# One core, a conditioned attention and MLP block: gate rows through memory, one token tile's maxima moved, the last products in another order

## The chip, the cores and the metric

The kernel runs on one core of one Trainium2 chip. The metric is the device time of one execution in microseconds (us), of the kernel before: median 770.49 of 3 runs (769.84 to 770.69).

## The reference

The block works on one sequence of S = 2048 tokens with D = 640 features, H = 32 heads of 20 features and an MLP of F = 1728. All inputs are float32.

```python
mod = (_silu(c) @ w_mod).reshape(c.shape[0], 6, 1, -1)
sa, ca, ga, sb, cb, gb = (mod[:, 0], ..., mod[:, 5])
h = _layernorm(x) * (1 + ca) + sa
# attention: q, k, v = h @ wqkv, per head
#   phi(u) = [softmax(u @ w_phi), softmax(-u @ w_phi)]
#   kv = phi_k^T v;  z = sum of phi_k over tokens
#   o = (phi_q kv) / (phi_q z + 1e-6);   A = o @ wo
x = x + ga * A
h = _layernorm(x) * (1 + cb) + sb
# MLP: r = max(h @ w1 + b1, 0);  B = (r * r) @ w2 + b2
x = x + gb * B
```

## The kernel before

**Numbers and tiles.** The tokens are cut into 16 tiles of 128 (index t), taken in 8 pairs (index j). Each float32 factor is split into a high part, rounded for TensorE, and a low part, the rest; a product is three matmuls (high by high, high by low, low by high). ScalarE writes the high part, VectorE subtracts it to get the low part (line 88, `lo`). So a product's third matmul, or its second, may wait for VectorE where its first waits for ScalarE.

**Stages.** Up to about 40 us weights are folded and the first tokens are normalized. Up to about 250 us a loop over t makes K, V and Q of each token tile (`proj`, tiles pk, pv, pq), the feature map's exponentials (ek, eq), and the sum kv (kvp). From about 250 to 385 us the attention output is made in a loop over j: TensorE turns the scaled features of a pair (ezb) in six groups (`tr_e`: tiles te 0 to 5, copied by ScalarE to ept 0 to 5; group 5 is the smallest, 80 rows), multiplies them with kv (`num`: tiles numa, numb, numc, for groups 0 and 1, 2 and 3, 4 and 5), and multiplies the outcome (ot) with wo (`do_wo`: pwo). ScalarE copies num's outcome as ot's high part (`num_hi`), VectorE makes ot's low part (`num_lo`). From 385 us on the MLP runs: for each pair j and each n = 0 to 6 two `up` products (f = 2n and 2n+1, h by w1, tile up), ReLU and square (ft), a split into ra, and the `down` products of an earlier n with w2 into accumulators. For the first pairs, and the last three n of the last pair, the down products are plain: four regions, named 2, 3, 4 and x, where 3 and x are the right 256 columns of the pair's two token tiles and 2 and 4 the left 384. Regions 3 and x lie in one bank of the accumulator memory (tile acc3x); 2 and 4 have one each.

**The gates and the other parts of mod.** mod has six parts of 640 numbers. `mod_mac(part, k)` adds row block k of w_mod, times silu(c), to a 128 by 640 sum on VectorE (tile wm), which needs one load of w_mod on SyncE's queue. A part that is wanted as a column (3 and 4, tile cols_b) is turned by five TensorE transposes (`mod_turn`: tile mc, or beside others in ta), copied by ScalarE (mt) and summed by VectorE (`mod_sum`). A part that is wanted as a row on all partitions (2 is the attention's gate, ga_b; 5 the MLP's, gb_b) is a matmul of the sum with a matrix of ones, in two halves (`mod_row`: tile mr, two matmul records each), and a copy on ScalarE.

**Order.** In the projection loop only TensorE's order is written out; a scheduler places the other engines' work. What is hung beside the loop stands in three tables by t: `SIDE`, `AFTER_KV` (behind the kv sum of a tile), and `LAST_COL` (the fifth transpose of a turn and its sum). From the attention loop on the order of all engines is the order of the program. VectorE's chain per pair there is the e' product with z (`e_prod`, into scr), its sums, and the scaling into ezb (`e_recip`, `e_scale`). Four token tiles are postponed or kept: their maxima, subtractions (`q_chain`) and exponentials are spread over j = 1, 3 and 5. In the MLP, tables `LN_AT0` to `LN_AT` say at which up product the next pair's adds and LN pieces are issued. The end is `last_downs`: the last n of the last pair, four regions, each with a gate multiply (`by_gate`), an add to y and a store.

Of the kernel before, what the change touches and what calls it, by code (L numbers as in the profile page):

```python
# [15 lines left out]
P = 128  # L16
S = 2048
D = 640
# [33 lines left out]
def kernel(  # L52
# [272 lines left out]
    def mod_row(part, dest, h, p=None):  # L325
        p = p or tp(f"mr{part}_{h}")
        c = slice(h * HALF, (h + 1) * HALF)
        nc.tensor.matmul(p[:, :HALF], ones, MA[part][:, c], start=True, stop=True)
        nc.scalar.activation(dest[:, c], p[:, :HALF], AF.Copy)
# [194 lines left out]
    def wo_weights(*gs):  # L524
# [4 lines left out]
        6: lambda: mod_turn(3, tp("mc3"), 0, 1, 2, 3),  # L529
        8: lambda: mod_row(2, ga_b, 0),  # L530
# [3 lines left out]
    LAST_COL = {7: (3, cols_b[:, 0:5]), 11: (4, cols_b[:, 5:10])}  # L534
    SIDE = {
        2: lambda: mod_mac(3, 0, 1, 2),
        3: lambda: (mod_mac(3, 3, 4), mod_mac(4, 0)),
        4: lambda: mod_mac(4, 1, 2),
        5: lambda: (mod_mac(4, 3, 4), mod_mac(2, 0)),
        6: lambda: mod_mac(2, 1, 2, 3),  # L540
        7: lambda: mod_mac(2, 4),
        8: lambda: None,
# [169 lines left out]
    for t in range(2, NT - 2):  # L712
        j, i = divmod(t, 2)
        if i == 0 and j < NT // 2 - 2:
            load_x(j + 2)
        PK[t] = row("s2", f"k{t}")
        to_sb(proj("k", t), PK[t])
        if t == NT - 4:
            t1(j + 1, 0, 1)
        if t == 9:  # L720
            mod_row(2, ga_b, 1)
        norm = j + 1 if i == 0 and t < NT - 4 else j + 2 if t == NT - 5 else None
        if norm:
            parts = ln_parts(XB[norm], f"a{norm}")
            with tc.issue_after(newest(ET_.Activation)):
                next(parts)
        p = proj("v", t, (1, 0, lambda: t1(j + 1, 4)) if t == NT - 3 else None)
        if i == 0:
            do_kv(t - 2)
            do_kv(t - 1)  # L730
            if t in AFTER_KV:
                AFTER_KV[t]()
        v_out(t, p)
        if norm:
            next(parts)
        EK[t] = tok2("k", f"ek{t}")
        spread(PK[t], EK[t], f"k{t}")
        exps(EK[t])
        if norm and not i:
            next(parts)  # L740
        if i and t < NT - 4:
            t1(j + 1, 2, 3)
        with tc.issue_after(newest(ET_.DVE)):
            k_norm(EK[t], t)
        if t < NT - POSTPONED:
            do_q(t, (1, 3, lambda: t1(j + 1, 4, more=LAST_COL.get(t))) if i else None)
            if norm and i:
                with tc.issue_after(newest(ET_.Activation)), tc.issue_after(DONE[0]):
                    next(parts)
            if i:  # L750
                with tc.issue_after(DONE[1]):
                    q_chain(t)
            else:
                q_chain(t)
        if i == 0 and t < NT - 4:
            t1(j + 1, 0, 1)
        SIDE[t]()
# [74 lines left out]
    def kv_diags():  # L832
# [3 lines left out]
        nc.tensor.transpose(kvt[1][:80, P : P + 40], kvs[:40, 600:680], ident[:40, :40])  # L836

# [275 lines left out]
    tr_e(0, range(3, NG))  # L1113
    mod_row(5, gb_b, 0, bank("mr5_0"))
    num(0)
    num_hi(0)
    mod_row(5, gb_b, 1, bank("mr5_1"))
# [11 lines left out]
    for j in range(NB):  # L1129
# [17 lines left out]
        def te(at):  # L1147
            for i, gs in enumerate((range(3), range(3, NG))):
                if nxt and te_at[i] == at:
                    tr_e(j + 1, gs)  # L1150
# [20 lines left out]
        if j == 3:  # L1171
            q_chain(KEPT + SPREAD[j], False)
# [17 lines left out]
        if j == 1:  # L1190
            q_chain(KEPT + SPREAD[j], False)
# [3 lines left out]
        if j in SPREAD:  # L1195
            exps(EQ[KEPT + SPREAD[j]])
        load_e(c + 2)
# [29 lines left out]
    def up(j, f):  # L1227

        n, k = FS[f], f % 2
        p = UP2[:, :256] if k and j < PLAIN else UP[:, 256 * k : 256 * k + 256]  # L1230
# [6 lines left out]
        mm(p, terms, first=(k == 0 or j < PLAIN), skip=True)  # L1237
# [204 lines left out]
    def last_downs(j):  # L1442
# [3 lines left out]
        for regs in ((("3", 0, R), ("x", 1, R)), (("2", 0, L),), (("4", 1, L),)):  # L1446
            for k in range(2):
                for r, i, c in regs:
                    f = NF - 2 + k
                    prod(j, r, block(j, NP - 1, (A11, A12, A21, A22)[2 * i + k]), W2[f], c, k == 1, FS[f])  # L1450
            for r, i, c in regs:
                m = c.stop - c.start
                t = u[:, at : at + m] if r != "4" else u[:, :m]
                at += m
                by_gate(t, acc(j, r)[1], c)
                add(Y[j][i][:, c], Y[j][i][:, c], t)
                store(j, i, c.start, c.stop)
# [11 lines left out]
    LN_AT2 = {"load": 0, "xx": 3, "add": (6, 7), "ln": (7, 8, 8, 8, 9, 9), 10: (0, 1), 11: (2, 3), 12: (4,)}  # L1469
# [45 lines left out]
    for j in range(NB):  # L1515
# [5 lines left out]
        for n in range(NP):  # L1521
            down = lambda k: prev and (down_plain if plain(*prev) else down_pair)(*prev, k)
            twice = not plain(j, n)
            m = NP * j + n - NP - 1
            done = j - 1 if j and prev else None
# [51 lines left out]
            if j == NB - 1 and n == NP - 1:  # L1577
                split_a(j, n, (0,))
                for i in range(2):
                    add(Y[j][i], Y[j][i], XR[j, i])  # L1580
# [3 lines left out]
            split_a(j, n, (0, 1) if (j, n) != (NB - 1, NP - 1) else (1,))  # L1584
# [89 lines left out]
```

## Time and profile before

| | |
|---|---|
| profiled execution, its own time | 770.42 us |
| its span, first to last instruction | 768.7 us |
| runs shown (3) | 769.84, 770.49, 770.69 us |
| mean clock granted to TensorE | 0.998 |
| TensorE matmuls busy | 760.7 us (99%) |
| VectorE busy | 591.4 us (77%) |
| ScalarE busy | 434.8 us (57%) |
| GpSimd busy | 146.8 us (19%) |

PE is TensorE's matmuls and PEld its weight loads, which run ahead of the matmuls; DVE is VectorE, ACT ScalarE, POOL GpSimd and SP SyncE. A row of a timeline has the start, the time from there to the end of the merged instructions, the engine, the line, the operation, what it writes and reads, and the number of instructions; in brackets stands how long the engine idled ahead of it, and what ended that. For weight loads, the distance between two starts is the time TensorE took for what lies between them.

### The profile page before, as it was taken

How to read it: one execution, taken by the hardware profiler on the slowest of the kernel's cores; microseconds unless marked ns; L12 is line 12 of the kernel's file. 1: busy time of each engine (PE TensorE's matmuls, PEld its weight loads, DVE VectorE, ACT ScalarE, POOL GpSimd, SP SyncE). 2: the span in 40 equal slices, each digit the busy share in tenths (PEclk: the TensorE clock that was granted, in tenths of full speed). 3: DMA queues.
4: the chain of work that ended last, by engine and by line, in shares of the span. 5: the costliest groups of instructions: out<-in, count | busy, mean ns of one | idle time of the engine just before them, and what ended most of it. 6: DMA issues, size and time to landing. Idle time of an engine off the chain costs nothing.

```text
span 768.7 us, 15287 instructions
## 1 busy us (share of the span) xinstructions
PE 760.7 (99%) x5965; PEld 740.3 (96%) x5965; DVE 591.4 (77%) x1081; ACT 434.8 (57%) x971; POOL 146.8 (19%) x301
## 2 busy tenths in 40 slices
PE   9999999999999999999999999999999999999997
PEld 9999999999999979988999999999999999999997
DVE  6698897968999899999556667866767666685656
ACT  5766756667853354556776647456463645546331
POOL 3001101202000255342101000222321313213110
PEclk9999999999999999999999999999999999999999
DMA  9711431512433355223356466897666759767450
GB/s 330 302 69 69 137 103 55 186 37 99 136 104 109 99 164 174 79 86 120 104 160 234 121 226 234 283 324 216 209 179 206 230 179 267 205 184 204 130 171 35
DMA packets 50551, 126.03 MB, mean 164 GB/s; under 512 B 5991, under 2 KB 6759, under 8 KB 50479
## 3 DMA queue, kind: packets, MB, share of 16 engines
q1 hardware_dynamic: 33144, 83.99, 31.8%
q0 software_dynamic: 14752, 35.76, 16.9%
q10 hardware_dynamic: 2583, 5.30, 1.8%
q8 instruction: 47, 0.77, 0.4%
q14 instruction: 25, 0.20, 0.1%
HBM read 95.05 MB, written 29.88 MB: 163 GB/s over the span
## 4 chain that ended last, share of the span: by engine, by line
PE 90%; DVE 4%; ACT 3%; DMA 1%; issue 1%; POOL 1%; SPq 0%; DVEq 0%; POOLq 0%; ACTq 0%
PE up L78 24%; PE acc L78 18%; PE pwo L78 10%; PE pk L78 7%; PE pq L78 7%; PE pv L78 6%; PE acc3x L78 5%; PE te L914 3%; PE kvp L450 2%; PE tb L357 1%; PE numa L78 1%; PE numb L78 1%; PE numc L78 1%; DMA wm<-in_w_mod 1%; PE foldk L280 1%
## 5 line engine op out<-in xcount | busy, mean ns | idle before, releaser
L78 PE MATMUL up<-h,w 128*128 128x256 f32 x1640 | 206.7, 278 | 0.2 <-ACT ft L1244 0.2
L78 PEld LDWEIGHTS up<-h,w 128*128 128x128 f32 x1640 | 196.2, 188 | 0.3 <-ACT ft L1244 0.3
L1244 ACT ACTIVATE ft<-up,b_t 128x256 f32<-128x256 f32 x104 | 48.8, 469 | 114.1 <-PE up L78 113.5
L78 PE MATMUL acc<-w,ra 128*128 128x384 f32 x452 | 98.0, 336 | 0.0
L1245 DVE TENSOR_TENSOR ft<-ft 128x256 f32<-128x256 f32 x104 | 44.1, 424 | 51.1 <-ACT ft L1244 49.5
L78 PE MATMUL pwo<-wo,ot 128*128 128x256 f32 (+3 forms) x512 | 81.1, 313 | 0.4 <-DVE ot L88 0.4
L78 PEld LDWEIGHTS pwo<-wo,ot 128*128 128x128 f32 (+1 forms) x512 | 74.4, 188 | 4.0 <-issue 2.7
L78 PE MATMUL pq<-wq,hT 128*128 128x384 f32 (+1 forms) x480 | 75.4, 312 | 0.0
L78 PEld LDWEIGHTS acc<-w,ra 128*128 128x128 f32 x452 | 72.7, 188 | 0.7 <-DVE ra L88 0.5
L78 PE MATMUL pk<-wk,hT 128*128 128x384 f32 (+1 forms) x480 | 72.7, 309 | 0.0
L78 PEld LDWEIGHTS pq<-wq,hT 128*128 128x128 f32 x480 | 71.2, 188 | 0.8 <-issue 0.2
L78 PE MATMUL pv<-wv,hT 128*128 128x384 f32 (+1 forms) x480 | 71.8, 307 | 0.0
L78 PEld LDWEIGHTS pk<-wk,hT 128*128 128x128 f32 x480 | 70.5, 188 | 0.4 <-issue 0.2
L78 PEld LDWEIGHTS pv<-wv,hT 128*128 128x128 f32 x480 | 70.0, 188 | 0.2
L88 DVE TENSOR_TENSOR ra<-ft,ra 128x384 fp32r<-128x384 f32 (+2 forms) x86 | 36.8, 449 | 32.9 <-ACT ra L1268 20.8
L78 PE MATMUL acc3x<-w,ra 128*128 128x256 f32 x248 | 42.4, 279 | 0.0
L1354 POOL DMA_DIRECT2D ring_a<-td_a x34 | 18.2, 536 | 124.7 <-PE acc L78 102.4
L1268 ACT ACTIVATE ra<-ft 128x384 fp32r<-128x384 f32 x48 | 25.2, 525 | 28.4 <-DVE ft L1245 22.4
L78 PEld LDWEIGHTS acc3x<-w,ra 128*128 128x128 f32 x248 | 39.8, 188 | 0.2 <-DVE ra L88 0.2
L878 POOL TENSOR_TENSOR dn<-dn,rs_q 128x32 f32<-128x32 f32 x32 | 22.6, 706 | 66.6 <-DVE dn L872 66.3
L441 DVE TENSOR_REDUCE sk<-ek 128x64 f32<-128x1280 f32 x16 | 23.7, 1483 | 13.9 <-ACT ek L436 13.4
L1259 DVE TENSOR_TENSOR ft<-ft 128x128 f32<-128x128 f32 x136 | 33.3, 286 | 1.2
(263 smaller groups left out, 1405.2 us busy)
## 6 DMA issues: line engine op xcount, KB each, us to landing
ring_c<-td_c POOLq DMA_DIRECT2D x34, 384.0 KB, 4.0
ring_a<-td_a POOLq DMA_DIRECT2D x34, 384.0 KB, 4.0
ring_b<-td_b POOLq DMA_DIRECT2D x34, 256.0 KB, 3.6
esp<-eq SPq DMA_DIRECT2D x12, 640.0 KB, 3.1
el<-esp SPq DMA_DIRECT2D x12, 640.0 KB, 5.3
rw<-in_w SPq DMA_DIRECT2D x23, 320.0 KB, 3.4
wm<-in_w_mod SPq DMA_DIRECT2D x20, 320.0 KB, 3.8
xb<-in_x SPq DMA_DIRECT2D x8, 640.0 KB, 4.0
```

What stands on the lines that cost most here:

```text
L78: nc.tensor.matmul(o, a, b, start=first and i == 0, stop=last and i == len(terms) - 1, skip_group_check=skip,)
L88: (eng or nc.vector).tensor_tensor(out_lo, full, hi.bitcast(F32), op=ALU.subtract)
L280: nc.tensor.matmul(p[g // 3][:, (g % 3) * 120 : (g % 3) * 120 + n], r, bd_t[:120, g * 120 : g * 120 + n], start=True, stop=True,)
L441: nc.vector.tensor_reduce(s, heads(flat(e)), axis=AX.X, op=ALU.add)
L450: nc.tensor.matmul(kvp[g // 4][64 * c : 64 * c + 64, a : a + 2 * n].rearrange("p (s n) -> p s n", s=2), v[:, u], e[:, :, o : o + n], start ...
L878: nc.gpsimd.tensor_tensor(dn[:, s], dn[:, s], rs[:, 1 - s], op=ALU.mult)
L914: nc.tensor.transpose(p[:m, a : a + P], EU[2 * j + i][:, b : b + m], ident)
L1244: nc.scalar.activation(r, p, AF.Relu, bias=b1_t[:, f : f + 1])
L1245: nc.vector.tensor_tensor(r, r, r, op=ALU.mult)
L1259: nc.vector.tensor_tensor(t[:, o], t[:, a], t[:, b], op=op)
L1268: nc.scalar.activation(a[:, 0, :3], t[:, :3], AF.Copy)
L1354: nc.gpsimd.dma_start(RING[j, n, r], TD[n][r].bitcast(F32R))
```

## The change

1. **Gate rows.** `mod_row` and its four calls go. The sums of parts 2 and 5 are turned and summed as the columns are (`mod_turn`, `mod_sum`), which gives a 128 by 5 tile (gate_a, gate_b). The new `spread_row` writes it to a small tensor in memory in the order of the features, and reads that back as a row on all 128 partitions; both transfers stand on SyncE's queue. The parts' order in the projection loop becomes 2, 3, 4. Part 5 is turned behind the kv transposes.
2. **Small block first.** `tr_e` takes groups 5, 3, 4 where it took 3, 4, 5.
3. **Maxima behind low parts.** At j = 3 `q_chain` moves from ahead of `num_lo(4)` to behind it, where it already stood for j = 1; behind it comes the sum and the spreading of gate b.
4. **LN passes.** In the projection loop, the LN passes of the later pairs are issued at another place (for the last pair two token tiles ahead). In the MLP, `LN_AT2` has its second add and two LN pieces earlier.
5. **The end.** The last two ups (12 and 13 of the last pair) stand back to back, the second in a bank of its own; then come the down products of n = 5 for regions 3, x and 2, then n = 6 for 3, x and 2, then n = 5 and 6 for 4. Each region is gated, added and stored behind its last product. The two adds of the residual (xr) stand ahead of the gate of 3.

```diff
-    def mod_row(part, dest, h, p=None):
-        p = p or tp(f"mr{part}_{h}")
-        c = slice(h * HALF, (h + 1) * HALF)
-        nc.tensor.matmul(p[:, :HALF], ones, MA[part][:, c], start=True, stop=True)
-        nc.scalar.activation(dest[:, c], p[:, :HALF], AF.Copy)
+    GD = [dram.tile([NC, P], F32, name=f"gate{h}") for h in range(2)]
+
+    def spread_row(h, col, dest):
+        nc.sync.dma_start(GD[h].rearrange("c p -> p c"), col)
+        nc.sync.dma_start(dest, GD[h].rearrange("c p -> (c p)")[None, :].to_broadcast([P, D]))
...
-        6: lambda: mod_turn(3, tp("mc3"), 0, 1, 2, 3),
-        8: lambda: mod_row(2, ga_b, 0),
+        6: lambda: mod_turn(2, tp("mc2"), 0, 1, 2, 3),
+        8: lambda: mod_turn(3, tp("mc3"), 0, 1, 2, 3),
...
-    LAST_COL = {7: (3, cols_b[:, 0:5]), 11: (4, cols_b[:, 5:10])}
+    LAST_COL = {7: (2, gate_a), 9: (3, cols_b[:, 0:5]), 11: (4, cols_b[:, 5:10])}
...
-        6: lambda: mod_mac(2, 1, 2, 3),
-        7: lambda: mod_mac(2, 4),
-        8: lambda: None,
+        6: lambda: mod_mac(4, 1, 2),
+        7: lambda: (spread_row(0, gate_a, ga_b), mod_mac(4, 3)),
+        8: lambda: mod_mac(4, 4),
...
-        if t == 9:
-            mod_row(2, ga_b, 1)
...
-            parts = ln_parts(XB[norm], f"a{norm}")
+            if not i:
+                parts = ln_parts(XB[norm], f"a{norm}")
...
-        if norm:
+        if norm and not i:
             next(parts)
...
+        if t == NT - 6:
+            parts = ln_parts(XB[j + 2], f"a{j + 2}")
+            with tc.issue_after(newest(ET_.Activation)):
+                next(parts)
         SIDE[t]()
...
+        mod_turn(5, kvt[1][:, 2 * P :], 4)
+        mod_turn(5, bank("mc5"), 0, 1, 2, 3)
...
-    tr_e(0, range(3, NG))
-    mod_row(5, gb_b, 0, bank("mr5_0"))
+    tr_e(0, (5, 3, 4))
     num(0)
     num_hi(0)
-    mod_row(5, gb_b, 1, bank("mr5_1"))
...
-            for i, gs in enumerate((range(3), range(3, NG))):
+            for i, gs in enumerate((range(3), (5, 3, 4))):
...
-        if j == 3:
-            q_chain(KEPT + SPREAD[j], False)
         do_wo(j, 1, 0)
...
-        if j == 1:
-            q_chain(KEPT + SPREAD[j], False)
...
         if j in SPREAD:
+            q_chain(KEPT + SPREAD[j], False)
             exps(EQ[KEPT + SPREAD[j]])
+        if j == 3:
+            mod_sum(5, gate_b)
+            spread_row(1, gate_b, gb_b)
...
-        p = UP2[:, :256] if k and j < PLAIN else UP[:, 256 * k : 256 * k + 256]
+        alone = j < PLAIN or (j, f) == (NB - 1, NF - 1)
+        p = UP2[:, :256] if k and j < PLAIN else tp("up13")[:, :256] if k and alone else UP[:, 256 * k : 256 * k + 256]
...
-        for regs in ((("3", 0, R), ("x", 1, R)), (("2", 0, L),), (("4", 1, L),)):
+        def part(n, r, i, c):
             for k in range(2):
-                for r, i, c in regs:
-                    f = NF - 2 + k
-                    prod(j, r, block(j, NP - 1, (A11, A12, A21, A22)[2 * i + k]), W2[f], c, k == 1, FS[f])
-            for r, i, c in regs:
-                m = c.stop - c.start
-                t = u[:, at : at + m] if r != "4" else u[:, :m]
-                at += m
-                by_gate(t, acc(j, r)[1], c)
-                add(Y[j][i][:, c], Y[j][i][:, c], t)
-                store(j, i, c.start, c.stop)
+                f = 2 * n + k
+                prod(j, r, block(j, n, (A11, A12, A21, A22)[2 * i + k]), W2[f], c, f == NF - 1, FS[f])
+
+        def out_(r, i, c, t):
+            by_gate(t, acc(j, r)[1], c)
+            add(Y[j][i][:, c], Y[j][i][:, c], t)
+            store(j, i, c.start, c.stop)
+
+        regs = ("3", 0, R), ("x", 1, R), ("2", 0, L), ("4", 1, L)
+        for r in regs[:3]:
+            part(NP - 2, *r)
+        for r in regs:
+            if r[0] == "4":
+                part(NP - 2, *r)
+                at = 0
+            part(NP - 1, *r)
+            m = r[2].stop - r[2].start
+            out_(*r, u[:, at : at + m])
+            at += m
...
-    LN_AT2 = {"load": 0, "xx": 3, "add": (6, 7), "ln": (7, 8, 8, 8, 9, 9), 10: (0, 1), 11: (2, 3), 12: (4,)}
+    LN_AT2 = {"load": 0, "xx": 3, "add": (6, 6), "ln": (7, 7, 8, 8, 9, 9), 10: (0, 1), 11: (2, 3), 12: (4,)}
...
+            if (j, n) == (NB - 1, NP - 1):
+                for k in range(2):
+                    up(j, 2 * n + k)
+                    split_a(j, n, (k,))
+                for i in range(2):
+                    add(Y[j][i], Y[j][i], XR[j, i])
+                break
...
-            if j == NB - 1 and n == NP - 1:
-                split_a(j, n, (0,))
-                for i in range(2):
-                    add(Y[j][i], Y[j][i], XR[j, i])
             up(j, 2 * n + 1)
```

The program's order shows the moves at three places. The first is VectorE at j = 3 in the attention loop, before: mxq and eq are the maxima and subtractions of a postponed tile, ot the low parts for j = 4, scr the e' product.

```order
L899 TENSOR_TENSOR ezb_3155<-el_3784,dn_3948 128x80
L430 TENSOR_REDUCE mxq_4055<-eq_2830 128x32
L431 TENSOR_REDUCE mxq_4055<-eq_2830 128x32
L433 TENSOR_TENSOR eq_2830<-eq_2830,mxq_4055 128x640 x2
L88 TENSOR_TENSOR ot_4080<-numa_4081,ot_4080 128x2x256
L88 TENSOR_TENSOR ot_4080<-numb_4082,ot_4080 128x2x256
L88 TENSOR_TENSOR ot_4080<-numc_4083,ot_4080 128x256
L88 TENSOR_TENSOR ot_4_4096<-numc_4083,ot_4_4096 40x256
L870 TENSOR_TENSOR scr_3157<-eq_2829,zb 128x1280
```

And the same place now:

```order
L906 TENSOR_TENSOR ezb_3165<-el_3797,dn_3961 128x80
L88 TENSOR_TENSOR ot_4088<-numa_4089,ot_4088 128x2x256
L88 TENSOR_TENSOR ot_4088<-numb_4090,ot_4088 128x2x256
L88 TENSOR_TENSOR ot_4088<-numc_4091,ot_4088 128x256
L88 TENSOR_TENSOR ot_4_4104<-numc_4091,ot_4_4104 40x256
L430 TENSOR_REDUCE mxq_4131<-eq_2840 128x32
L431 TENSOR_REDUCE mxq_4131<-eq_2840 128x32
L433 TENSOR_TENSOR eq_2840<-eq_2840,mxq_4131 128x640 x2
L310 TENSOR_REDUCE gate_b<-mt_3229 128x5
L877 TENSOR_TENSOR scr_3167<-eq_2839,zb 128x1280
```

The four low parts stand ahead of the maxima, and the sum of gate b is new between these and the e' product.

The second is TensorE around the first num of the attention loop, before (mr is a gate half, kvd the sum kv):

```order
L914 MATMUL te_4_3317<-ident,ezb_3153 120x128 x2
L914 MATMUL te_5_3324<-ident,ezb_3152 80x128
L914 MATMUL te_5_3324<-ident,ezb_3153 80x128
L328 MATMUL mr_0_3329<-wm_4_2822,ones 128x320
L78 MATMUL numa_3333<-ept_0_3281,kvd 64x256 x2
```

And now:

```order
L921 MATMUL te_5_3329<-ident,ezb_3162 80x128
L921 MATMUL te_5_3329<-ident,ezb_3163 80x128
L921 MATMUL te_3_3334<-ident,ezb_3162 120x128 x2
L921 MATMUL te_3_3334<-ident,ezb_3163 120x128 x2
L921 MATMUL te_4_3341<-ident,ezb_3162 120x128 x2
L921 MATMUL te_4_3341<-ident,ezb_3163 120x128 x2
L78 MATMUL numa_3349<-ept_0_3300,kvd 64x256 x2
```

The gate half is gone, and group 5 is turned ahead of groups 3 and 4.

The third is TensorE's end, with what each row waits for, before. In w_10 to w_13 the number is f; acc3x holds regions 3 and x, the other two accumulators 2 and 4.

```order
L78 MATMUL up<-h_7_8699,w_13_5009 128x256 x9
L78 MATMUL acc_7_9013<-w_10_5053,ra_5_9345 128x384 x2
L78 MATMUL acc_7_9013<-w_10_5053,ra_5_9345 128x384 [waits DVE_49]
L78 MATMUL acc3x_9060<-w_10_5053,ra_5_9345 128x256 x3
L78 MATMUL acc_7_9013<-w_11_5096,ra_5_9345 128x384 x3
L78 MATMUL acc3x_9060<-w_11_5096,ra_5_9345 128x256 x3
L78 MATMUL acc3x_9060<-w_12_5144,ra_6_9392 128x256 [waits Activation_49]
L78 MATMUL acc3x_9060<-w_12_5144,ra_6_9392 128x256
L78 MATMUL acc3x_9060<-w_12_5144,ra_6_9392 128x256 [waits DVE_49]
L78 MATMUL acc3x_9060<-w_12_5144,ra_6_9392 128x256 [waits Activation_49]
L78 MATMUL acc3x_9060<-w_12_5144,ra_6_9392 128x256
L78 MATMUL acc3x_9060<-w_12_5144,ra_6_9392 128x256 [waits DVE_49]
```

And now, from the last pair's region 3 on:

```order
L78 MATMUL acc3x_9076<-w_12_5160,ra_6_9396 128x256 [waits Activation_49]
L78 MATMUL acc3x_9076<-w_12_5160,ra_6_9396 128x256
L78 MATMUL acc3x_9076<-w_12_5160,ra_6_9396 128x256 [waits DVE_49]
L78 MATMUL acc3x_9076<-w_13_5163,ra_6_9396 128x256 [waits DVE_49]
L78 MATMUL acc3x_9076<-w_13_5163,ra_6_9396 128x256
L78 MATMUL acc3x_9076<-w_12_5160,ra_6_9396 128x256 [waits DVE_49]
L78 MATMUL acc3x_9076<-w_12_5160,ra_6_9396 128x256 x2
L78 MATMUL acc3x_9076<-w_13_5163,ra_6_9396 128x256 x2
L78 MATMUL acc_7_9025<-w_12_5160,ra_6_9396 128x384 x3
L78 MATMUL acc_7_9025<-w_13_5163,ra_6_9396 128x384 x2
L78 MATMUL acc_7_9029<-w_10_5069,ra_5_9361 128x384 x3
```

Region 3 is finished in the first five rows; the sixth row is the first product of x, whose wait is for VectorE's gate multiply of region 3. Before, the products of 3 and x were mixed, and none of them waited for a gate.

More of the change, by code (lines that the diff above doesn't have):

```diff
@@ L533 @@
     }
-    LAST_COL = {7: (3, cols_b[:, 0:5]), 11: (4, cols_b[:, 5:10])}
+    gate_a = const.tile([P, NC], F32, name="gate_a")
+    gate_b = const.tile([P, NC], F32, name="gate_b")
+    LAST_COL = {7: (2, gate_a), 9: (3, cols_b[:, 0:5]), 11: (4, cols_b[:, 5:10])}
     SIDE = {
[L536 to L539, printed above, removed]
-        6: lambda: mod_mac(2, 1, 2, 3),
-        7: lambda: mod_mac(2, 4),
-        8: lambda: None,
+        2: lambda: mod_mac(2, 0, 1, 2),
+        3: lambda: (mod_mac(2, 3, 4), mod_mac(3, 0)),
+        4: lambda: mod_mac(3, 1, 2),
+        5: lambda: (mod_mac(3, 3, 4), mod_mac(4, 0)),
+        6: lambda: mod_mac(4, 1, 2),
+        7: lambda: (spread_row(0, gate_a, ga_b), mod_mac(4, 3)),
+        8: lambda: mod_mac(4, 4),
         9: lambda: wo_weights(0, 1),
@@ L1236, in up @@
                 terms += [(W1[f][:, 0, d], H2[j][:, d, 0]), (W1[f][:, 0, d], H2[j][:, d, 1])]
-        mm(p, terms, first=(k == 0 or j < PLAIN), skip=True)
+        mm(p, terms, first=(k == 0 or alone), skip=True)
         if k == 0:
@@ L1583 @@
                 down(1)
-            split_a(j, n, (0, 1) if (j, n) != (NB - 1, NP - 1) else (1,))
+            split_a(j, n)
             if twice:
```

## The prediction

> **What bounds the kernel now.** I read the page first (engines, chain), then what the weight-load side of TensorE waits for, then the order of time around those waits.
>
> ```profile
> PE 760.7 (99%) x5965; PEld 740.3 (96%) x5965; DVE 591.4 (77%) x1081; ACT 434.8 (57%) x971; POOL 146.8 (19%) x301
> ...
> PE 90%; DVE 4%; ACT 3%; DMA 1%; issue 1%; POOL 1%; SPq 0%; DVEq 0%; POOLq 0%; ACTq 0%
> ```
>
> TensorE is the bound: 760.7 of 768.7 us, 90% of the chain. Only shorter TensorE work, its few waits, and the end that is left to VectorE can move the time. One row of the table by stretches, from the attention loop (us; then busy time of PE, PEld, DVE, ACT, POOL), shows the limit on that, and one row of the waits the only wait of the MLP that matters here:
>
> ```profile
> 280.00:300.00 20.00, 19.97 (x151) 18.43 (x150) 19.48 (x25) 11.07 (x24) 13.95 (x24) 1.00 0.49 151
> ```
> ```profile
> PEld up L78 <- ACT ft L1244: 0.3, 1, 0.3
> ```
>
> VectorE is busy 19.48 of 20 us there, so what TensorE gains comes through only as far as VectorE moves too. The profiled execution took 770.42 us and the median is 770.49, 0.07 apart; I count against 770.42 and take the result for the median. About 0.2%, 1.54 us, is what a measurement of this kernel can tell from no change.
>
> **Step 1, gate rows in the projection loop.** Weight loads in order of time: t=6 (four mc transposes between kvp and pq), t=8 (first mr half in that place), then t=9 (second half between pk and pv) and t=10 (nothing there).
>
> ```profile
> 120.00 2.38 PEld L450 LDWEIGHTS kvp<-ek,vt 128*64 128x64 f32 x44
> ...
> 122.85 3.32 PEld L78 LDWEIGHTS pq<-wq,hT 128*128 128x128 f32 x20
> ...
> 150.41 2.38 PEld L450 LDWEIGHTS kvp<-ek,vt 128*64 128x64 f32 x44
> ...
> 153.48 2.56 PEld L78 LDWEIGHTS pq<-wq,hT 128*128 128x128 f32 x14
> ...
> 158.42 4.45 PEld L78 LDWEIGHTS pk<-wk,hT 128*128 128x128 f32 x30
> ...
> 167.66 0.46 PEld L357 LDWEIGHTS ta<-ident,xb 128*128 128x128 f32 x4
> ...
> 172.70 4.37 PEld L78 LDWEIGHTS pk<-wk,hT 128*128 128x128 f32 x30
> ...
> 181.50 1.58 PEld L450 LDWEIGHTS kvp<-ek,vt 128*64 128x64 f32 x31
> ```
>
> From kvp to pq it is 3.07 us with an mr half and 2.85 with four transposes, which now stand at both: -0.22. From pk to the end of pv it is 9.24 us with the half and 8.80 without: -0.44. The four transposes take 0.47 (2.85 less the 2.38 of kvp), 0.12 each, and one more goes into t=9's ta bank: +0.12. Step 1 gives -0.54. The added VectorE reduce at t=7 and the two transfers of gate a have no user for long; they count nothing here, and rival 3 prices the transfers.
>
> **Step 2, the LN passes of the last pair.** They now run earlier on ScalarE, the first two (L337) ahead of k's second half and of eq.
>
> ```profile
> 194.58 0.74 ACT L436 ACTIVATE eq<-eq 128x640 f32<-128x640 f32 x1 [1.91 <-DVE eq L433]
> ...
> 195.49 0.73 ACT L337 ACTIVATE xb<-xb 128x640 f32<-128x640 f32 x1
> ...
> 202.25 0.20 PEld L357 LDWEIGHTS ta<-ident,xb 128*128 128x128 f32 x2 [0.84 <-ACT hfa L368]
> ...
> 203.55 0.76 DVE L88 TENSOR_TENSOR hT<-hfa,hT 128x256 fp32r<-128x256 f32 x2 [1.80 <-ACT hT L369]
> ```
>
> ScalarE idles 1.91 us ahead of eq, so two passes of 0.73 go into idle time, and hfa, for which TensorE waited 0.84, comes by that much earlier: -0.84. VectorE waited 1.80 at 203.55 for what hangs on the same copy, so it can follow. Steps 1 and 2 make -1.38 by 250 us, for TensorE and for VectorE. The bounds of step 2 are 0 (the passes only change places) and -0.84; I take the upper one, since the idle time is longer than both passes.
>
> **Step 3, the attention loop.** In order of time, VectorE, ScalarE and the weight loads:
>
> ```profile
> 303.02 0.69 DVE L88 TENSOR_TENSOR ot<-numa,ot 128x512 fp32r<-128x512 f32 x1 [0.30 <-ACT ot L943]
> ...
> 304.60 0.75 DVE L88 TENSOR_TENSOR ot<-numc,ot 128x256 fp32r<-128x256 f32 x2 [0.24 <-ACT ot L943]
> ...
> 332.34 0.81 DVE L430 TENSOR_REDUCE mxq<-eq 128x32 f32<-128x640 f32 x1
> ...
> 335.51 0.68 DVE L88 TENSOR_TENSOR ot<-numa,ot 128x512 fp32r<-128x512 f32 x1
> ...
> 337.37 1.47 DVE L870 TENSOR_TENSOR scr<-eq,zb 128x1280 f32<-128x1280 f32 x1
> ...
> 349.08 0.68 DVE L88 TENSOR_TENSOR ot<-numa,ot 128x512 fp32r<-128x512 f32 x1
> ```
> ```profile
> 333.53 0.66 ACT L943 ACTIVATE ot<-numc 128x256 fp32r<-128x256 f32 x2 [0.27 <-PE numc L78]
> ```
> ```profile
> 333.41 2.13 PEld L78 LDWEIGHTS pwo<-wo,ot 128*128 128x128 f32 x18 [0.39 <-issue]
> 336.25 1.87 PEld L78 LDWEIGHTS pwo<-wo,ot 128*128 128x128 f32 x11 [0.70 <-DVE ot L88]
> ...
> 348.76 0.54 PEld L78 LDWEIGHTS pwo<-wo,ot 128*128 128x128 f32 x4 [0.39 <-issue]
> ...
> 375.38 0.63 PEld L78 LDWEIGHTS numa<-ept,kvd 120*64 120x64 f32 x8 [0.29 <-ACT ept L916]
> ```
>
> At j=0 five transposes come in (0.6 by step 1) and two mr halves and waits for ept_5 go, so TensorE stands better there by more than it keeps: VectorE has its first wait since 256 us at 303.02, and only its two waits for ScalarE, 0.30 and 0.24, can come out of its row. So at j=2 both engines stand at -1.38 - 0.54 = -1.92. At j=3 the maxima and subtractions (332.34 to 335.51, 3.17 us) leave the place ahead of the low parts, and TensorE's wait of 0.70 for these goes: -2.62. VectorE now does the low parts once ScalarE's highs are there, 334.19 - 1.92 = 332.27, ends the last half of that pair 0.37 later, 332.6, then does the 3.17, 335.8, and the new reduce, 336.6 (0.81, as the first row of that chain). So the e' product starts 0.8 ahead of 337.37, not 1.92 ahead, and all behind it likewise: the first low part of j=4 ends at 349.76 - 0.8 = 349.0. TensorE needs it after 18 loads, as at j=3: 348.76 + 2.13 - 2.62 = 348.3. So a new wait of 0.7 us appears at j=4, and -1.92 is left. Of the wait of 0.29 at the last num, I take -0.2, since te 5 is now copied first. After the loop: -2.1.
>
> **Step 4, the earlier add in the MLP.** It hands ScalarE its LN pass sooner; of the wait of 0.3 for ft I take -0.2 (bounds 0 and -0.3): -2.3.
>
> **Step 5, the tail**, from up 12 on:
>
> ```profile
> 753.82 1.78 PEld L78 LDWEIGHTS up<-h,w 128*128 128x128 f32 x15
> ...
> 755.52 0.47 PEld L78 LDWEIGHTS acc<-w,ra 128*128 128x128 f32 x3
> ...
> 757.01 0.29 ACT L1274 ACTIVATE ra<-ft 128x128 fp32r<-128x128 f32 x1
> ...
> 757.55 1.55 DVE L1409 TENSOR_TENSOR y<-y,xr 128x640 f32<-128x640 f32 x2
> ...
> 758.68 0.47 ACT L1248 ACTIVATE ft<-up,b_t 64x256 f32<-64x256 f32 x1 [1.38 <-PE up L78]
> ...
> 760.54 0.42 DVE L88 TENSOR_TENSOR ra<-ft,ra 64x256 fp32r<-64x256 f32 x1 [0.49 <-ACT ra L1278]
> ...
> 761.47 1.68 PEld L78 LDWEIGHTS acc<-w,ra 128*128 128x128 f32 x10
> ...
> 761.78 0.42 DVE L1412 TENSOR_TENSOR end<-acc3x,gb_b 128x256 f32<-128x256 f32 x1 [0.82 <-PE acc3x L78]
> ...
> 765.01 0.56 DVE L1409 TENSOR_TENSOR y<-y,end 128x384 f32<-128x384 f32 x1
> ```
>
> Up 12 takes 1.70 us for 15 loads, 0.113 each, which I use for products 256 wide, and 1.5 times that, 0.17, for 384 wide (ten took 1.68). On before's clock: up 13 now issues right behind up 12, until 755.52 + 1.13 = 756.65. Then regions 3, x and 2 of the older pair, 0.68 + 0.68 + 1.04, until 759.05, and 3 of the last pair, 0.57, until 759.62. ScalarE is busy with part 12 until 757.30 and makes ft 13 by 757.77; the rest of that part took 760.96 - 759.15 = 1.81, so its low part ends at 759.58. Now VectorE does the two adds of xr (1.55) until 761.13, and only then the gate of 3 (0.42), until 761.55. The halves 3 and x lie in one bank, and the first x product of the last pair now waits for that gate in the program; before, both halves were done ahead of the first gate. So TensorE stops from 759.62 to about 761.6, 2 us, then does x 0.57, 2 0.86 and all eleven of 4, 1.90: 764.93. The gate of 4 starts 0.31 behind that, as 761.78 behind 761.47, and with its add takes 1.14 (0.55 + 0.03 + 0.56): 766.38 against 765.57, **+0.8**.
>
> Had x gone straight on, TensorE would be done at 762.95, and VectorE's eight passes (761.78 to 765.57, 3.79), right behind the adds, at 764.9: -0.7. The Trainium skill (PSUM — Partial Sum Buffer, PSUM bank collisions) says that the chip doesn't arbitrate between TensorE and VectorE on one bank, and that semaphores should guard by bank and quadrant, not by address; by this rule the stop is needed and the sum has +0.8, by a guard on addresses it would have -0.7. The trace of before can't show it.
>
> **Sum:** -0.54 - 0.84 - 0.54 - 0.70 + 0.70 - 0.2 - 0.2 + 0.8 = -1.5, so 770.42 - 1.5 = **768.9 us**.
>
> **Rivals.**
> 1. *The tail's stop does not bite* (x goes on): -0.7 in place of +0.8, so 767.4. For it: 3 is ready early, so that its gate could be long done if VectorE were free. Against: the two adds are queued ahead of that gate. 0.13.
> 2. *VectorE eats the gain.* ScalarE's earlier passes delay others as much as they help hfa. Then both engines stand at -0.54 - 0.54 = -1.08 at j=2; at j=3 the low parts end at 333.5, the 3.17 and the reduce at 337.5, and the e' product doesn't move at all. TensorE, at -1.78, needs the low part of j=4 at 349.1 and gets it at 349.76: -1.1 is left, with -0.4 and +0.8 it is -0.7: 769.7. For it: the 19.48 of 20; against: the 1.80 of idle time at 203.55. 0.27.
> 3. *Slower: the gate's transfers hold SyncE's queue.* The write of gate a puts 640 single values of 4 bytes to memory, the broadcast read waits for it, and behind both stands the load of the last w_mod piece of that part of the loop. The nearest rows (the slowest transfer of this stage; a reduce like gate a's, one tile ahead of it in time; the hT low parts, behind which VectorE now uses that piece):
>
> ```profile
> el<-esp SPq DMA_DIRECT2D x12, 640.0 KB, 5.3
> ```
> ```profile
> 143.81 0.82 DVE L310 TENSOR_REDUCE cols_b<-mt 128x5 f32<-128x640 f32 x1
> ...
> 162.86 0.75 DVE L88 TENSOR_TENSOR hT<-hfa,hT 128x256 fp32r<-128x256 f32 x2
> ```
>
> Even at 5.3 us each, write, read and load end at 144.6 + 15.9 = 160.5, ahead of 163.5. It decides from 3 us more on. If the small values make the write take 10 us (twice the row), it is 165.2, and VectorE stops 1.7; if they make it 14, VectorE stops 5.7 ahead of the q subtractions, TensorE with it but for the 1.80 of slack, and the time is 768.9 + 3.9 = 772.8. The Trainium skill (DMA: Bandwidth & Descriptors, Rules for kernel authors) says that a strided last dim lowers to one descriptor per element, which speaks for it; no row here shows such a write. 0.12.
> 4. *The forecast.* 0.48.
>
> **Numbers.** The forecast's own unknowns are the new wait at j=4 (0 to 1.4) and the tail's stop (0.8, half a microsecond either way), so 767.9 to 770.1. The range takes in rival 1 with that half microsecond, rival 2, and the near part of rival 3: 766.9 to 771.5. Faster by over 0.2% means below 768.95: somewhat over half of the forecast (0.27), rival 1, and a little of rival 2 (0.03): 0.43. Slower by over 0.2% is above 772.0: most of rival 3 and what I don't see: 0.14. Between them 0.43.
>
> **What would show it.** Right: no wait of ta for hfa near 202; VectorE's maxima behind the low parts at j=3; a wait of pwo for ot of under 1.5 us at j=4; in the tail a wait of acc3x for VectorE's gate of about 2 us, and the last add some 0.8 us later behind up 12 than before. Wrong: that wait missing, the e' product of j=3 at 337.4 or later, or a VectorE wait for wm near 163.

## The result and the profile after

The changed kernel takes 769.68 us in the median of 14 runs (768.51 to 771.06), the kernel before 770.34 beside it (14 runs, 769.06 to 771.26): the ratio is 0.9992, with an interval of 0.9984 to 1.0001. That is 0.66 us less, within the 0.2% that the prediction named, where it had put the gain at 1.5. The profiled execution of the changed kernel took 769.86 us, 0.56 less than that of before.

The page first, then what TensorE's weight loads wait for (us in total, times, longest):

```profile
PE 759.3 (99%) x5967; PEld 739.8 (96%) x5967; DVE 593.8 (77%) x1083; ACT 434.6 (57%) x971; POOL 144.2 (19%) x301
...
PE 85%; DVE 8%; issue 2%; DMA 2%; POOL 2%; ACT 1%; SPq 0%; POOLq 0%; DVEq 0%
```
```profile
PEld acc3x L78 <- DVE end L1418: 1.6, 1, 1.6
PEld pwo L78 <- DVE ot L88: 1.1, 2, 0.9
...
PEld acc L78 <- DMA ring_b<-td_b: 0.9, 1, 0.9
PEld te L921 <- ACT ept L923: 0.9, 2, 0.5
```

TensorE has 1.4 us less work, and four longer waits that are new. Two were forecast: the stop of x in the tail, and the wait for the low part at j = 4. Two were not: for a transfer (ring_b), and, at j = 2, for ScalarE's copies of the turned features (te for ept). VectorE's share of the chain went from 4% to 8%. In order of time, the weight loads that answer to those shown of before:

```profile
200.98 0.24 PEld L357 LDWEIGHTS ta<-ident,xb 128*128 128x128 f32 x2
...
309.82 0.16 PEld L921 LDWEIGHTS te<-ident,ezb 128*80 128x80 f32 x2 [0.54 <-ACT ept L923]
...
331.73 4.57 PEld L78 LDWEIGHTS pwo<-wo,ot 128*128 128x128 f32 x32 [0.39 <-issue]
...
349.55 2.39 PEld L78 LDWEIGHTS pwo<-wo,ot 128*128 128x128 f32 x14 [0.89 <-DVE ot L88]
...
373.91 0.63 PEld L78 LDWEIGHTS numa<-ept,kvd 120*64 120x64 f32 x8 [0.17 <-ACT ept L925]
...
515.61 0.41 PEld L78 LDWEIGHTS acc<-ring_b,rs 128*128 128x128 f32 x3 [0.88 <-DMA ring_b<-td_b]
515.96 1.13 PEld L78 LDWEIGHTS up<-h,w 128*128 128x128 f32 x9
...
752.66 2.91 PEld L78 LDWEIGHTS up<-h,w 128*128 128x128 f32 x25
...
760.42 0.64 PEld L78 LDWEIGHTS acc3x<-w,ra 128*128 128x128 f32 x5 [1.63 <-DVE end L1418]
```

There is no wait at ta (0.84 before), none at j = 3 (0.70 before), where all 32 loads run through, and 0.89 at j = 4. At j = 2 te waits 0.54, and 0.33 more at its next loads (310.31), where it had no wait before. ScalarE's exponentials of j = 2, which stand ahead of the copies that te waits for:

```profile
306.91 0.74 ACT L436 ACTIVATE eq<-eq 128x640 f32<-128x640 f32 x1 [2.99 <-DVE eq L433]
```

ScalarE waits for VectorE's subtractions there, and from there to the copies (309.18) it has no idle time: TensorE meets VectorE's limit by way of ScalarE. VectorE at j = 3 and 4, and in the tail:

```profile
333.21 0.80 DVE L430 TENSOR_REDUCE mxq<-eq 128x32 f32<-128x640 f32 x1
...
336.37 0.81 DVE L310 TENSOR_REDUCE gate_b<-mt 128x5 f32<-128x640 f32 x1
337.10 1.48 DVE L877 TENSOR_TENSOR scr<-eq,zb 128x1280 f32<-128x1280 f32 x1
...
348.82 0.68 DVE L88 TENSOR_TENSOR ot<-numa,ot 128x512 fp32r<-128x512 f32 x1
...
758.48 1.56 DVE L1415 TENSOR_TENSOR y<-y,xr 128x640 f32<-128x640 f32 x2
759.96 0.42 DVE L1418 TENSOR_TENSOR end<-acc3x,gb_b 128x256 f32<-128x256 f32 x1
...
764.66 0.56 DVE L1415 TENSOR_TENSOR y<-y,end 128x384 f32<-128x384 f32 x1
```

In the tail the two adds (758.48 to 760.04) stand ahead of the gate of 3 (759.96), and x starts behind it, at 760.42. From up 12 (752.66) to the last add's end (765.22) it is 12.56 us; before it was 11.75.

The start of the same load in both profiles, after less before, shows where time came and went. Both kernels do the same up to 100 us, but the first loads came 0.40 later in this profile (over all runs below this point scatters by about 1 us), so that is taken off.

| place | measured step | forecast |
|---|---|---|
| t = 8 and 9, mr halves gone | -0.79 | -0.54 |
| ta at 202 us, wait gone | -0.88 | -0.84 |
| kept at j = 2 (te at 311.8) | -1.92 in all | -1.92 in all |
| j = 3, wait gone | -0.87 | -0.70 |
| j = 4, new wait and what leads to it | +1.05 | +0.70 |
| last num | 0 | -0.2 |
| 470 to 505 us, steps of under 0.2, cause open | -0.4 | 0 |
| ring_b at 515 us, new wait | +0.80 | 0 |
| ft at 517 us, wait gone | -0.42 | -0.2 |
| 520 to 720 us, small steps, cause open | +0.20 | 0 |
| tail, up 12 to the last add | +0.81 | +0.8 |

From the row of j = 2 on, which holds the two above it, the measured steps add up to -0.75 and those of the forecast to -1.52.

### The profile page after: what moved, and what is told of

Same layout as the page of the kernel before. It is cut to its first block, busy times and chain, and to the rows that moved or that the text cites. A ratio compares the mean times of both kernels' runs of the same rounds, so it can differ in the third digit from the quotient of the medians.

```text
span 768.2 us, 15300 instructions
## 1 busy us (share of the span) xinstructions
PE 759.3 (99%) x5967; PEld 739.8 (96%) x5967; DVE 593.8 (77%) x1083; ACT 434.6 (57%) x971; POOL 144.2 (19%) x301
## 2 busy tenths in 40 slices
DMA packets 52151, 126.69 MB, mean 165 GB/s; under 512 B 7335, under 2 KB 8103, under 8 KB 52079
## 4 chain that ended last, share of the span: by engine, by line
PE 85%; DVE 8%; issue 2%; DMA 2%; POOL 2%; ACT 1%; SPq 0%; POOLq 0%; DVEq 0%
PE up L78 23%; PE acc L78 17%; PE pk L78 9%; PE pv L78 9%; PE pq L78 8%; PE pwo L78 5%; PE acc3x L78 5%; PE kvp L450 3%; DVE dn L879 2%; DVE scr L877 2%; DVE ezb L901 1%; PE tb L357 1%; PE te L921 1%; DMA ring_b<-td_b 1%; PE ta L357 1%
## 5 line engine op out<-in xcount | busy, mean ns | idle before, releaser
L885 POOL TENSOR_TENSOR dn<-dn,rs_q 128x32 f32<-128x32 f32 x32 | 20.1, 629 | 68.1 <-DVE dn L879 67.8
```

The costliest lines, as they stand in the source:

```text
L885: nc.gpsimd.tensor_tensor(dn[:, s], dn[:, s], rs[:, 1 - s], op=ALU.mult)
```

## The experiments

My theory behind the table: the tail's stop, the transfers that LN_AT2 brings together, and the sum of gate b on a VectorE that has no idle time, take back what the gate rows and the LN passes give. The rivals stand with each run. A run's time is a median of 5 to 11 executions that spread over 0.5 to 2.6 us, and the kernel before, timed beside them, was between 770.30 and 770.49. Of differences under about 0.5 us only the rows of the profiles can tell.

**The end of the kernel before.** `last_downs`, the last ups and the adds as before.

```diff
-            if (j, n) == (NB - 1, NP - 1):
-                for k in range(2):
-                    up(j, 2 * n + k)
-                    split_a(j, n, (k,))
-                ...
+            if j == NB - 1 and n == NP - 1:
+                split_a(j, n, (0,))
+                for i in range(2):
+                    add(Y[j][i], Y[j][i], XR[j, i])
```

> The changed kernel with the end of the kernel before (up 13 behind the older pair's products, 3 and x mixed, the adds of xr where they were). Theory: the stop of x for the gate of 3 makes the new end 0.8 us longer from up 12 to the last add (12.56 against 11.75), so with the old end that stretch is 11.75 again, and the time is 0.8 below the changed kernel: 768.9. Rival (the new end is no worse, and the 0.8 is scatter of one profile): the stretch stays at 12.4 or more, or the time does not move, 769.7.

768.51 us, 1.17 below the changed kernel. The loads of up 12 and VectorE's last add in this run:

```profile
752.98 1.77 PEld L78 LDWEIGHTS up<-h,w 128*128 128x128 f32 x15
```
```profile
764.17 0.56 DVE L1414 TENSOR_TENSOR y<-y,end 128x384 f32<-128x384 f32 x1
```

That is 11.75 us again. The tail's loss of 0.8 is real; a little more came in the median.

**LN_AT2 as before.**

```diff
-    LN_AT2 = {..., "add": (6, 6), "ln": (7, 7, 8, 8, 9, 9), ...}
+    LN_AT2 = {..., "add": (6, 7), "ln": (7, 8, 8, 8, 9, 9), ...}
```

> The changed kernel with LN_AT2 of the kernel before. Theory: the earlier second add brings the store of x and the reload of xr forward, into the time in which ring_b is fetched at 508 to 515, and the wait of acc for ring_b (0.88) comes from that; with the old table it is gone and the wait of up for ft (0.35) is back: TensorE 0.4 to 0.5 earlier from 520 us on, 769.2. Rival (the whole kernel runs 1.5 us earlier against its transfers, whatever the table; the wait is luck of that): a wait for ring_b of 0.5 or more stays, and ft's comes on top: 769.9.

769.15 us, 0.53 below. Weight loads at the same place:

```profile
514.23 0.41 PEld L78 LDWEIGHTS acc<-ring_b,rs 128*128 128x128 f32 x3
514.99 1.78 PEld L78 LDWEIGHTS up<-h,w 128*128 128x128 f32 x15 [0.35 <-ACT ft L1250]
```

No wait for ring_b, and ft's is back, as the theory had it. The issues on SyncE's queue show what the table moves; first the changed kernel, then the kernel before:

```profile
507.09 1.05 SPq L1081 DMA_DIRECT2D x<-xm  x2
508.20 2.10 SPq L1405 DMA_DIRECT2D xr<-x  x2
```
```profile
508.96 4.30 SPq L1074 DMA_DIRECT2D x<-xm  x2
513.31 1.03 SPq L1399 DMA_DIRECT2D xr<-x  x2
```

With the second add early, both stores and both reloads are issued within 3.2 us, just as ring_b is fetched; before, the second store came 4 us later. What ring_b's fetches took from issue to landing between 495 and 520 us, in the changed kernel and in this run:

```profile
DMA to landing us min/median/max: 3.5/4.7/7.4
```
```profile
DMA to landing us min/median/max: 3.6/4.5/5.5
```

The longest is the fetch that is issued 1 us behind the first store. In the nine profiles with both adds at 6 the fetch beside the stores took 6.2 to 7.6 us; in the five with the adds at 6 and 7 (before, and four of the runs) it took 4.8 to 5.7. So transfers that are issued together do slow the fetch, by 0.5 us at least. How much of that TensorE waits for is not fixed: from none to 1.10 with both adds at 6, none in the five. The LN piece that moved with the add has no part in it: the table moves one (only its second entry differs, not two as the change was described), and the last run below keeps that one early and has no such wait. Where the transfers meet stays open.

**The sum of gate b on ScalarE.** The copies of the five turned blocks also sum them.

```diff
-        mod_turn(5, ...)                  # copies by ScalarE
+        for i, c in enumerate(cs_):
+            nc.scalar.activation(t[:, c * P : (c + 1) * P], p[:, i * P : (i + 1) * P],
+                                 AF.Identity, accum_out=dest[:, c : c + 1])
...
-            mod_sum(5, gate_b)
```

> The changed kernel with the sum of gate b taken on ScalarE, in the copies of its five turned blocks, so that VectorE has no reduce (0.81) at j = 3. Theory: VectorE is the limit there and TensorE's new wait at j = 4 (0.9 us of pwo for ot at 349) comes from that reduce: it falls to 0.1 or 0.2 and all behind is 0.7 earlier: 769.0. Rival (the maxima chain behind the low parts is late by itself, or TensorE is stopped by other things right behind): the wait stays above 0.5, or goes and comes back before 385 us, and the time is 769.5 or more.

776.67 us: 7.0 above the changed kernel, for a reason that neither had named. The issues on SyncE's queue, and VectorE:

```profile
261.99 0.38 SPq L336 DMA_DIRECT2D gate<-gate_b  x1
262.42 0.53 SPq L1015 DMA_DIRECT2D rw<-in_w  x1
263.16 0.33 SPq L875 DMA_DIRECT2D el<-esp  x1
272.35 0.33 SPq L337 DMA_DIRECT2D gb_b<-gate  x1
272.77 0.38 SPq L875 DMA_DIRECT2D el<-esp  x1
```
```profile
276.29 1.49 DVE L885 TENSOR_TENSOR scr<-el,zb 128x1280 f32<-128x1280 f32 x1 [6.76 <-DMA el<-esp]
```

In the attention loop the program fixes the order of the other engines, but SyncE's is left to the scheduler. The sum was now ready at 262 us, so the write of the gate was placed there, and the read behind it held the queue until 272.35. An el load stood behind the read, and VectorE waited 6.76 us for it. This is the prediction's slower rival, at the other gate. TensorE's loads then stood for 4.4 us, up to 282.69, and behind that its clock was halved for some us (the last three numbers of the row are the granted clock, the share of the DMA engines and GB/s):

```profile
286.00:288.00 2.00, 2.00 (x9) 2.00 (x8) 2.00 (x2) 0.87 (x2) 0.79 (x1) 0.50 0.76 257
```

So the lag of TensorE is more than its waits. The wait at j = 4 did fall, from 0.89 to 0.2.

**The sum on ScalarE with the write held at j = 3.**

```diff
-            mod_sum(5, gate_b)
+            nc.vector.tensor_scalar(gate_b, gate_b, 1.0, None, op0=ALU.mult)
             spread_row(1, gate_b, gb_b)
```

> The sum of gate b on ScalarE again, but its write to memory held at j = 3, where the changed kernel has it, by a multiply by 1.0 of the 128 by 5 tile on VectorE (0.11 us). Theory: the 7 us of the run before this one came only from the write, which SyncE's queue then waited for ahead of an el load; held back, what is left is the shorter wait at j = 4 (0.9 to 0.1): 0.7 below the changed kernel, 769.0. Rival (the five ScalarE copies with sums are what cost, ahead of eq and kvd): te and num at 266 to 275 us come later by 0.3 or more and the time is 769.7 or above.

768.58 us, 1.1 below the changed kernel. At j = 4:

```profile
348.54 2.39 PEld L78 LDWEIGHTS pwo<-wo,ot 128*128 128x128 f32 x14 [0.25 <-DVE ot L88]
```

The wait went from 0.89 to 0.25, and what stands behind it came 0.7 earlier, up to ring_b, whose wait was 1.10 here: the reduce of 0.81 made 0.64 of that wait.

**The maxima ahead of the low parts again.**

```diff
+        if j == 3:
+            q_chain(KEPT + SPREAD[j], False)
         do_wo(j, 1, 0)
```

> The changed kernel with the maxima chain of j = 3 ahead of the low parts again, the sum of gate b staying. Theory: VectorE does the same work up to the e' product in either order, so the wait of about 0.7 at j = 3 comes back, VectorE stays at most 0.5 behind, and the wait at j = 4 shrinks by about as much: TensorE within 0.3 of the changed kernel at 360 us, 769.7. Rival (the move is a gain of its own, 0.9, with the wait at j = 4 due to the reduce alone): waits at both places and 770.4.

768.93 us. At j = 3 and j = 4:

```profile
334.11 2.39 PEld L78 LDWEIGHTS pwo<-wo,ot 128*128 128x128 f32 x14 [0.69 <-DVE ot L88]
...
346.63 4.57 PEld L78 LDWEIGHTS pwo<-wo,ot 128*128 128x128 f32 x32 [0.39 <-issue]
```

The wait moves from j = 4 back to j = 3, and TensorE stands 0.2 better behind both: with the reduce on VectorE the move of the chain is worth nothing. The rest of the 0.75 in the median lies elsewhere: in this profile ring_b's wait is 0.20, which gives 0.6 more.

**The adds of xr one pair of ups earlier.**

```diff
+            if (j, n) == (NB - 1, NP - 2):
+                for i in range(2):
+                    add(Y[j][i], Y[j][i], XR[j, i])
             split_a(j, n)
```

> The changed kernel with the two adds of xr one pair of ups earlier, in VectorE's idle time behind up 11, so that they no longer stand ahead of the gate of 3. Theory: the stop of x (1.63 us) is the gate of 3 queued behind the adds; it falls to about 0.8 (the gate itself and its hand-over, 0.31 + 0.42 and what comes with it), and the end is 0.8 earlier: 768.9. Rival (the stop is the price of the shared bank alone, the adds have time): the stop stays above 1.4, 769.7.

768.68 us, 1.0 below. The first x of the last pair:

```profile
758.78 0.66 PEld L78 LDWEIGHTS acc3x<-w,ra 128*128 128x128 f32 x5 [0.72 <-DVE end L1418]
```

The stop falls from 1.63 to 0.72: 0.9 of it was the queue on VectorE, the rest is the gate of the shared bank. This profile also has no wait for ring_b, so the 1.0 in the median may not be the tail's alone.

**Regions in the order 3, 2, x, 4**, with the early adds.

```diff
-        for r in regs:
+        for r in (regs[0], regs[2], regs[1], regs[3]):
```

> As the run with the early adds, and the last pair's regions in the order 3, 2, x, 4: the products of 2 (0.86 us) stand between the last product of 3 and the first of x. Theory: the gate of 3 is done in that time, no stop is left (0.1 at most), and the end is 1.6 to 1.9 earlier than in the changed kernel: 768.0. Rival (VectorE's eight passes of gate and add, 3.8 us, set the end instead): the end is only 1.0 earlier, with VectorE without a gap up to the last add: 768.7.

767.99 us. Up 12, the first x, and the last add:

```profile
751.82 2.91 PEld L78 LDWEIGHTS up<-h,w 128*128 128x128 f32 x25
...
758.68 0.70 PEld L78 LDWEIGHTS acc3x<-w,ra 128*128 128x128 f32 x5
```
```profile
762.12 0.56 DVE L1415 TENSOR_TENSOR y<-y,end 128x384 f32<-128x384 f32 x1
```

No stop is left, and the tail takes 10.86 us, 1.70 less than in the changed kernel and 0.89 less than before: the new end gains, once the gate of 3 has something to hide behind.

**The LN passes of the projection loop as before.**

```diff
-            if not i:
-                parts = ln_parts(XB[norm], f"a{norm}")
+            parts = ln_parts(XB[norm], f"a{norm}")
```

> The changed kernel with the LN passes of the projection loop where the kernel before had them. Theory: the wait of ta for hfa at 202 us (0.84) comes back, VectorE's hT low parts come 0.8 later and VectorE has no gap from there on to make it up, so the whole rest is 0.8 later: 770.4. Rival (VectorE is late by itself up to 303 us, TensorE's 0.84 is slack by then): the wait comes back, but the shift is gone by 312 us: 769.7.

769.22 us. The wait did not come back, so neither theory held. ScalarE's last step of the pair ahead, in the kernel before's place and here:

```profile
185.31 0.92 ACT L348 ACTIVATE xb<-xb,nba,sqa 128x640 f32<-128x640 f32 x1 [1.36 <-POOL nba L345]
```
```profile
183.16 1.74 ACT L348 ACTIVATE xb<-xb,nba,sqa 128x640 f32<-128x640 f32 x2
```

Before, ScalarE waited 1.36 us for GpSimd there; here, and in the changed kernel, it doesn't, and hfa is ready in time with the passes at either place. That the median is 0.46 lower says nothing of the passes: in the profile 0.3 of it is ring_b's wait.

**The LN passes alone**, in the kernel before.

```diff
+            if not i:
+                parts = ln_parts(XB[norm], f"a{norm}")
-            parts = ln_parts(XB[norm], f"a{norm}")
```

> The kernel before with nothing changed but the place of the LN passes in the projection loop. In the run before this one these passes stood at their old place and the wait of ta for hfa was gone all the same; there, and in the changed kernel, ScalarE no longer waits 1.36 us for GpSimd's nba at 183 to 185 us. Theory A (either is enough: ScalarE has 2.5 us of idle time that the passes can fill): the wait at 202 is gone or under 0.2, and all behind is 0.8 earlier up to the place where VectorE is the limit: 769.6. Theory B (only GpSimd's being on time counts): the wait stays at 0.5 or more, 770.4.

769.50 us, a ratio of 0.9990 (0.9981 to 0.9999) to the kernel before. ScalarE and the loads of ta:

```profile
185.19 1.74 ACT L348 ACTIVATE xb<-xb,nba,sqa 128x640 f32<-128x640 f32 x2 [1.36 <-POOL nba L345]
```
```profile
201.21 0.24 PEld L357 LDWEIGHTS ta<-ident,xb 128*128 128x128 f32 x2
```

GpSimd's delay is there, and the wait at ta is gone all the same. Either removes it; in the changed kernel the second of them found nothing left to remove.

**Gate a written in rows.** One more transpose, and the write has 5 rows of 512 bytes.

```diff
+        nc.tensor.transpose(p[:NC, :P], gate_a, ident)
+        nc.scalar.activation(gate_r, p[:NC, :P], AF.Copy)
+        nc.sync.dma_start(GD[0], gate_r)
```

> The changed kernel with gate a turned once more on TensorE (one transpose, 128 by 5 to 5 by 128) and copied by ScalarE, so that it is written to memory as 5 rows of 512 bytes where the changed kernel writes 640 single values, which took 9.9 us until the read behind it could start. Theory (the time of that write goes with the number of pieces): the read is issued 2 to 3 us behind the write. Rival (it is the wait for the write to be confirmed, whatever its shape): 8 us or more. In both the time stays within 0.4 of 769.7, since nothing waits for ga_b before 181 us.

The waits of SyncE's queue (us, times, longest), in the changed kernel and here:

```profile
SPq L329 <- DMA gate<-gate_b: 10.5, 1, 10.5
...
SPq L329 <- DMA gate<-gate_a: 9.5, 1, 9.5
```
```profile
SPq L542 <- DMA gate<-gate_r: 0.8, 1, 0.8
```

The read waited 0.8 us for the write where it had waited 9.5: the time goes with the 640 pieces. On the pages, the packets of under 512 bytes are 5991 before, 7335 in the changed kernel with its two writes, and 6684 here. The Trainium skill (DMA: Bandwidth & Descriptors, Rules for kernel authors) says that a strided last dim lowers to one descriptor per element; these runs agree, with their own numbers. The kernel's time missed the forecast, at 772.28 us: the transpose stood in TensorE's order behind the mc transposes and waited for ScalarE,

```profile
155.40 0.08 PEld L539 LDWEIGHTS gr<-ident,gate_a 128*5 128x5 f32 x1 [2.12 <-ACT mt L306]
```

and TensorE stood 3.8 us later from there on. The wait was 2.12 of that; most of the rest came behind it, where the granted clock fell to about half (1.00 at this place in the changed kernel):

```profile
157.00:159.00 2.00, 2.00 (x8) 2.00 (x8) 1.93 (x3) 0.00 (x0) 0.00 (x0) 0.51 0.16 65
```

The loads of pq were 0.32 us apart there, and 0.18 in the changed kernel.

**All that helped together:** early adds and 3, 2, x, 4; LN_AT2 as before; the sum on ScalarE with its write held.

> The changed kernel with what the runs so far were for: adds of xr early and regions in the order 3, 2, x, 4; LN_AT2 of the kernel before; the sum of gate b on ScalarE with the write held at j = 3. Theory (the three lie in different stages and add up: 1.7, 0.5 and 0.7 us): 2.9 below the changed kernel, 766.8. Rival (what is gained at j = 4 is lost where the transfers of the MLP meet again, or VectorE's last passes set the end): 767.6 or more.

766.89 us, a ratio of 0.9953 (0.9941 to 0.9966) to the kernel before: 2.8 below the changed kernel and as forecast. The parts lie in different stages and add up.

**The same with only one LN pass of LN_AT2 early.**

```diff
-    "add": (6, 7), "ln": (7, 8, 8, 8, 9, 9)
+    "add": (6, 7), "ln": (7, 7, 8, 8, 9, 9)
```

> As the run with all three, but LN_AT2 keeps its new place for one LN pass (the second at 7) with both adds at their old place (6 and 7). Theory: the store of x stays spread, so no wait for ring_b, and ScalarE is free for ft earlier, so that wait (0.35) goes too: 0.3 below the run with all three. Rival (the pass at 7 delays what ScalarE owes there): no gain or a wait of up or acc of 0.3.

767.16 us (0.9955, 0.9942 to 0.9967): no gain. The wait for ft moves one pair of ups ahead and grows:

```profile
511.49 1.83 PEld L78 LDWEIGHTS up<-h,w 128*128 128x128 f32 x15 [0.59 <-ACT ft L1258]
```

## Why the prediction was right, and where not

The time lies in the range, and the change is one that a measurement can't tell from none, which had 0.43 of the chance, as much as the gain. The point that it named, 768.9, was 0.78 too low. By the steps of the table 0.77 are missing: 0.58 in step 4, 0.2 each at the last num and between 520 and 720 us, 0.18 at j = 3 and 4, against which 0.4 came unforecast between 470 and 505 us. By its steps:

- **Step 1** held in kind; the mr halves were worth 0.79 rather than 0.54.
- **Step 2** had the right size, 0.88 for 0.84, for a cause that was only half of it. The passes alone do remove the wait, but so did GpSimd's being on time, which came with the rest of the change. Why GpSimd's three small steps took 3.0 us before and 1.6 after stays open; the orders of its instructions differ around them only by two fills.
- **Step 3** was right where it mattered: the gain of TensorE at the first num (1.7 us) shrank to VectorE's own, 1.92 in all at j = 2, by the two waits of te for ScalarE. VectorE stood 1.34 earlier ahead of its two waits for ScalarE (300.16 for 301.10) and 2.02 behind them (302.98 for 304.60), with the 0.40 taken off; the forecast was 1.38 and 1.92. The reading that VectorE had no wait between 256 and 303 us was wrong: it waited 0.27 and 0.69 us for GpSimd, at 264.79 and 275.11, but the changed kernel has the same two waits, so nothing came of it. The 0.70 that the chain's move gave came back as a wait at j = 4. That wait was 0.89, for a forecast of 0.7, and 0.64 of it is the reduce. Rival 2 had put the e' product of j = 3 where it was; it started 0.67 earlier (337.10 for 337.37, less the 0.40), for a forecast of 0.8.
- **Step 4** is the step that failed. I looked at ScalarE's order alone, and not at the transfers that hang on the moved add. The term was -0.2; the runs show -0.42 for ft and 0 to 1.1 for ring_b, +0.80 in this profile, so +0.38 together. With the old table the median fell by 0.53. That is most of the 0.78 between the forecast and the median.
- **Step 5** was right, +0.81 for +0.8, with a stop of 1.63 for 2. The early adds and the other order show both halves of its mechanism, the queue ahead of the gate and the shared bank; the Trainium skill (PSUM — Partial Sum Buffer, PSUM bank collisions) has semaphores guard by bank and quadrant and not by address, and the trace agrees: x lies in other columns of the bank than the gate of 3 reads, and x waited 1.63, so rival 1 is out. No run here went without that guard.
- **The slower rival** had the mechanism and the wrong bound: the write took twice the slowest row that I had (9.5 and 10.5 us until the read could go, for 5.3). Gate a's piece of w_mod was still issued at 156.11 and used at 161.98, so nothing waited; the same kind of write placed ahead of an el load cost 7 us. Its price for a stop of TensorE had only the wait itself in it; the two long waits of these runs also brought a halved clock.

## What to carry to other kernels

Before a product is moved ahead so that its result can be used early, look at who shares its bank and what is queued on the engine that frees it; another region's products put in between make the wait free. A gain on the engine that bounds the kernel passes only as far as its partner has idle time, so count each new instruction on the partner as a wait. Look for that wait also on a third engine: here TensorE met VectorE's limit through ScalarE. When a step is moved, follow its transfers as well: two stores and two reloads issued together delayed a third party's fetch by at least 0.5 us.

## What the runs showed of the hardware

A write of 2.5 KB as 640 single values kept the read behind it waiting for 9.5 and 10.5 us, and with it what stood behind that read on the queue; as 5 rows of 512 bytes it was 0.8.

A fetch of 256 KB issued 1 us behind the first of two stores and two reloads of 320 KB took 6.2 to 7.6 us where all four were issued within 2.5 us, and 4.8 to 5.7 where the second store came 4 us behind the first.

Behind waits of 2.12 and 4.4 us TensorE's granted clock was about 0.5 for some us (0.51 at 157 to 159, 0.50 at 286 to 288); behind the stops of the changed kernel, of 1.63 and less, it stayed 1.00.
